# Gated attention plus S4 convolution on one core: a reordered prologue, zero fills by DMA, and new costs in the planner that writes the instruction orders

## The chip, the cores and the metric

The kernel runs on one core of one Trainium2 chip. The metric is the device time of one execution in microseconds (us); lower is better. The core has TensorE (PE, matmuls, with its weight loads shown apart as PEld), VectorE (DVE), ScalarE (ACT), GpSimd (POOL) and SyncE (SP). Each runs its own instruction stream in order and waits on semaphores. DMA transfers are issued from an engine's stream (here from SP) and run on 16 shared DMA engines.

## The reference: what is computed

```python
x = A_x                                              # (1, 2048, 448), bf16
g = sigmoid((x * gate_w).sum(-1, keepdims=True))
# A: attention, 16 query heads of 28, one shared key and value head
q, k, v = heads(x @ wq), x @ wk, x @ wv
a = concat(softmax(q @ k.T * 28 ** -0.5) @ v) @ wo
# B: a state-space (S4) convolution along the sequence, per channel d, 256 modes n
dt = exp(log_dt)
K[d, l] = Re sum_n C[d, n] * dt B[d, n] * exp(dt A[d, n] * l)
b = causal_conv(x, K) + x * Dskip                    # by FFT of length 4096
out = g * a + (1 - g) * b
```

## The kernel before

**Who sets the order.** The kernel does not issue its instructions where they stand in the code. Each `pg.op(engine, fn, ns, rd, wr, pr, ...)` notes an operation, its estimated duration `ns`, the keys it reads and writes, and a priority `pr` (smaller goes first). `Prog.schedule` (L113) then simulates the five engines: again and again it takes, of all operations whose inputs are ready, the one that can start first, and among equals the one with the smallest `pr`. This gives each engine a fixed order; `emit` adds the semaphore waits. `slack` is a delay that the planner adds before it holds an operation for ready; a `lock` guards a PSUM bank used in turn by several operations. A DMA is booked (L105) at packets x (30 + 0.03 x bytes) ns / 16 x 1.1, or packets x (105 + 0.022 x bytes) / 16 x 1.1 from 1500 bytes on, one after the other, then 2200 ns until it has landed; its issue takes 60 ns of the queue (L171). If a transfer lands later than planned, the engine that comes to it stands still with all that follows in its order.

**Prologue.** Four DMAs bring x into `tab` (key `xst`). PE transposes it in two halves (L475) through banks 0 to 3, ACT and DVE copy it to `xT` (L486, L488). ACT also writes the zeros of `U` (L393) and DVE those of `O` (L394) and of the padded weights (L384). `prep_params` (L493) makes the seeds of the S4 kernel: transposed parameters (L517), range reduction, sine and cosine by ACT (L535, L536), products (L523, the helper line of all of them). `prep_attn` (L562) makes `kT` (L571, L576), its largest magnitude (L579) and from that the column `Wb` that bounds the exponent (L585), the values (L592, L596) and the gates (L609, L615, L617, L620). A DMA (`omq`, L623) brings 1 - g into rows of 64, and PE mirrors and spreads them (L630). `qproj` (L638) makes the queries of one group of four heads: four matmuls (L649), absolute values (L655), the `Wb` matmul (L657), the copy to `qT` (L659).

**Attention.** 16 steps of (512 queries, 4 heads). For 1024 tiles PE makes scores (L915) in batches of 3 and 2, ACT takes the exponential (L925, 410 instructions), and PE multiplies by V (L933, "P.V", four matmuls of one key block). `norm` (L877) ends a step: DVE copies (L883), a DMA brings the row sums to `denT` (four pieces, L885), DVE inverts them (L888), they go through DRAM (`R_scratch`) and come back as `rdenB` (L890), and DVE multiplies (L892). `outp` (L850) makes the output projection.

**Convolution.** 28 chunks of 16 channels. DVE builds powers in `masters` (L694 to L709, once for four chunks) and `tables` (L722 to L757). `kgen` (L760) contracts them on PE (L773, four groups of 16 matmuls) in the bank `psX`, DVE copies to `kstg` (L783), and four DMAs write the kernel values to DRAM, `KP_scratch` (L786). For each of four channel quads, `tload` (L790) reads a Toeplitz layout of 1 MB back into one of three `T` buffers, and PE runs 8 steps of four matmuls (L829) against `U`, the blocks of x loaded by 48 DMAs (`uload`, L445). DVE takes the result to `cst` (L837), PE transposes it (L807), DVE adds it to `O` (L814). The convolution of a chunk is noted two chunks behind its kernel generation (`LAG`).

Of the kernel before, what the change touches and what calls it, by code (L numbers as in the profile page):

```python
# [11 lines left out]
P = 128  # L12
# [41 lines left out]
class Prog:  # L54
# [44 lines left out]
    def dma(self, pairs, desc, slot, rd=(), wr=(), pr=0, eng="sp", slow=False):  # L99
        kw = dict(allow_slow_non_contiguous=True) if slow else {}  # L100

        def fn(e):
            return [e.dma_start(o, i, **kw) for o, i in pairs]  # L103
        nd, size = desc
        o = self.op(eng, fn, nd * (30.0 + 0.03 * size if size < 1500 else 105.0 + 0.022 * size) / 16.0 * 1.1, rd, wr, pr)  # L105
        o.slot, o.ndma = slot, len(pairs)
        prev = self.slots.get(slot)
        if prev is not None:
            o.deps[prev] = 1
        self.slots[slot] = o.i  # L110
        return o

    def schedule(self):  # L113
# [19 lines left out]
        while done < n:  # L133
# [148 lines left out]
def el(n, rate=0.96, fix=62):  # L282
    return fix + n / rate


class Kernel:
# [10 lines left out]
    def build(self):  # L297
        nc = self.nc
        with self.es:
# [5 lines left out]
            self.prep_params()  # L305
            self.prep_attn()
            self.main()
# [4 lines left out]
    def alloc(self):  # L312
# [51 lines left out]
        self.KP = nc.dram_tensor("KP_scratch", (D * KPW,), BF).ap()  # L364
        self.R = nc.dram_tensor("R_scratch", (16 * 4 * 512,), F32).ap()

    def consts(self):
# [16 lines left out]
        ms = lambda buf, n, val, key: pg.op("dve", lambda e: e.memset(V(buf, 0, n), val), 60 + n / 3.8, wr=[key])  # L384
        ms(self.Wq, NT * 512, 0.0, "Wq")
        ms(self.Wk, NT * P, 0.0, "Wk")
        ms(self.Wo, NT * D, 0.0, "Wo")
        ms(self.Wb, P, 0.0, "Wb")
        pg.op("dve", lambda e: e.memset(self.vaug.v(0, P, 28, [[32, 16]]), 1.0), 80, wr=["va"])
        pg.op("dve", lambda e: e.memset(self.vaug.v(0, P, 29, [[32, 16], [1, 3]]), 0.0), 80, wr=["va"])  # L390
        pg.op("dve", lambda e: e.memset(V(self.zero, 0, 1), 0.0), 60, wr=["zero"])
        zz = self.zero.v(0, P, 0, [[0, 16 * D]])
        pg.op("act", lambda e: e.activation(self.U.v(0, P, 16 * D, [[1, 16 * D]]), zz, AF.Copy), 6200, rd=["zero"], wr=["Uz"])  # L393
        pg.op("dve", lambda e: e.memset(V(self.O, 0, 16 * D), 0.0), 3000, wr=["O"], pr=1)  # L394
# [6 lines left out]
        pg.op("dve", lambda e: e.memset(V(self.kstg, 0, 256), 0.0), 100, wr=[("kst", 0)])  # L401

    def loads(self):
# [3 lines left out]
        for hf in range(4):  # L407
            pg.dma([(xst.v(0, P, hf * 4 * D, [[D, 4], [1, D]]), dram(x, hf * 4 * P * D, [[D, P], [P * D, 4], [1, D]]))],
                   (512, 896), f"x{hf}", wr=[("xst", hf)], eng="sp")
# [4 lines left out]
        def lraw(k):  # L414
            pg.dma([(self.rawv(k, DT, 0, [[NM, 4], [1, NM]]), dram(ins[self.names[k]], 0, [[NM, DT], [DT * NM, 4], [1, NM]]))],
                   (448, 512), f"raw{k}", wr=[("raw", k)])
        pg.dma([(wks.v(0, DT, 0, [[DH, 4], [1, DH]]), dram(ins["A_wk"], 0, [[DH, DT], [DT * DH, 4], [1, DH]])),
                (self.Wv.v(0, DT, 0, [[32, 4], [1, DH]]), dram(ins["A_wv"], 0, [[DH, DT], [DT * DH, 4], [1, DH]]))],
               (896, 56), "wk", wr=["wks", "Wv"])
        pg.op("dve", lambda e: e.tensor_copy(self.Wk.v(0, DT, 0, [[32, 16], [1, DH]]),  # L420
                                             wks.v(0, DT, 0, [[DH, 4], [0, 4], [1, DH]])), 300, rd=["wks"], wr=["Wk", "rd"])
        lraw(0)
        lraw(1)
        pg.dma([(self.dt32.v(0, P, 0, [[1, D]]), dram(ins["B_log_dt"], 0, [[0, P], [1, D]]))], (128, 896), "ldt", wr=["dt"])
# [3 lines left out]
                                             wst.v(0, DT, 0, [[DH, 64], [1, DH]])), 1000, rd=["wqs"],  # L428
              wr=["Wq", ("acc", 0), ("acc", 1)])
# [3 lines left out]
        for k in range(2, 6):  # L433
            lraw(k)
# [3 lines left out]
        pg.dma([(dram(self.KP, 4 * S, [[4 * KPW, 112], [1, 256]]), self.kstg.v(0, 112, 0, [[1, 256]]))],  # L438
               (112, 512), "pad", rd=[("kst", 0)], wr=["pad"], eng="sp", pr=3)
# [5 lines left out]
    def uload(self):  # L445
        pg, x = self.pg, self.ins["A_x"]
        for k in range(3):
# [7 lines left out]
            pg.dma(lst, (1024, 896), f"u{k}", rd=["sw", "Uz"], wr=["U"], pr=2)  # L455
# [10 lines left out]
    def prep_x(self):  # L466
        pg = self.pg
        xst, xT = self.tab, self.xT
        for hf in range(2):
            for T in range(NT):  # L470
                t, o = self.bank(T, True)

                def mm(e, hf=hf, T=T, t=t, o=o, part=0):
                    for k in range(4 * part, 4 * part + 4):
                        r = e.matmul(t.v(0, DT, o + 128 * k, [[1, 128]]),  # L475
                                     xst.v(0, P, (8 * hf + k) * D + DT * T, [[1, DT]]),
                                     self.ident.v(0, P, 0, [[1, P]]), is_transpose=True, tile_position=(0, 0))
                    return r
                for part in range(2):
                    pg.op("pe", lambda e, mm=mm, part=part: mm(e, part=part), 450,  # L480
                          rd=[("xst", 2 * hf + part), "id"], wr=[("b", T)])
                dst = xT.v(0, DT, T * S + 1024 * hf, [[1, 1024]])
                src = t.v(0, DT, o, [[1, 1024]])
                key = f"xT{T}" + "ab"[hf]
                if T % 2 == 0:
                    pg.op("act", lambda e, d=dst, s=src: e.activation(d, s, AF.Copy), 1030, rd=[("b", T)], wr=[key], pr=-2)  # L486
                else:
                    pg.op("dve", lambda e, d=dst, s=src: e.tensor_copy(d, s), 700, rd=[("b", T)], wr=[key], pr=-2)  # L488

    def xk(self, col, c=None):  # L490
        return [f"xT{T}" + ("a" if col < 1024 else "b") for T in range(NT)]

    def prep_params(self):  # L493
        pg = self.pg
        fT, fO = self.T.cast(F32), self.U.cast(F32)
        W2 = 2 * D
        fb = lambda j: (fT, j * W2) if j < 6 else (fO, (j - 6) * W2)
        t = lambda j: fb(j)[0].v(0, P, fb(j)[1], [[1, W2]])
        tt = lambda j: fb(j)[0].v(0, P, fb(j)[1], [[D, 2], [1, D]])
        tc = lambda j: fb(j)[0].v(0, P, fb(j)[1], [[D, 2], [16, NCH], [1, 16]])  # L500
        f = fT
        K = lambda j: ("tp", j)
        allT = [("T", s) for s in range(self.NTR)]
        dtb = self.dt32.v(0, P, 0, [[0, 2], [1, D]])
        pg.op("act", lambda e: e.activation(f.v(0, P, 0, [[1, D]]), self.dt32.v(0, P, 0, [[1, D]]), AF.Exp), 600,
              rd=["dt"], wr=[K(0)], pr=1.3)
        pg.op("dve", lambda e: e.tensor_copy(self.dt32.v(0, P, 0, [[1, D]]), f.v(0, P, 0, [[1, D]])), 400,
              rd=[K(0)], wr=["dt"], pr=1.3)
        bk = {0: 4, 1: 5, 2: 6, 3: 4, 4: 5, 5: 6}

        def trans(k):
            t_, o = self.bank(bk[k], True)

            def mm(e):
                for half in range(2):
                    for T in range(4):
                        r = e.matmul(t_.v(0, P, o + half * D + DT * T, [[1, DT]]),  # L517
                                     self.rawv(k, DT, T * NM + 128 * half, [[1, 128]]),
                                     self.ident.v(0, DT, 0, [[1, DT]]), is_transpose=True, tile_position=(0, 0))
                return r  # L520
            pg.op("pe", mm, 800, rd=[("raw", k), "id"] + [("on", i) for i in range(2)], wr=[("b", bk[k])], pr=1.4)
            return t_.v(0, P, o, [[D, 2], [1, D]]), ("b", bk[k])
        TT = lambda e, o, a, b, op: e.tensor_tensor(o, a, b, op)  # L523
        ns = el(W2)
        p0, k0 = trans(0)
        p1, k1 = trans(1)
        pg.op("dve", lambda e: TT(e, tt(0), p0, dtb, ALU.mult), ns, rd=[k0, "dt"], wr=[K(0)] + allT, pr=1.3)
        pg.op("dve", lambda e: TT(e, tt(1), p1, dtb, ALU.mult), ns, rd=[k1, "dt"], wr=[K(1)], pr=1.3)
        pg.op("act", lambda e: e.activation(t(0), t(0), AF.Exp), 950, rd=[K(0)], wr=[K(0)], pr=1.3)
        pg.op("dve", lambda e: e.tensor_scalar(t(2), t(1), 1.0 / TWO_PI, MAGIC, ALU.mult, ALU.add), ns / 2, rd=[K(1)], wr=[K(2)], pr=1.3)  # L530
        pg.op("dve", lambda e: e.tensor_scalar(t(2), t(2), -MAGIC, -TWO_PI, ALU.add, ALU.mult), ns / 2, rd=[K(2)], wr=[K(2)], pr=1.3)
        pg.op("dve", lambda e: TT(e, t(1), t(1), t(2), ALU.add), ns, rd=[K(1), K(2)], wr=[K(1)], pr=1.3)
        pg.op("dve", lambda e: e.tensor_scalar(t(1), t(1), -math.pi, math.pi, ALU.max, ALU.min), ns / 2, rd=[K(1)], wr=[K(1)], pr=1.3)
        pg.op("dve", lambda e: e.scalar_tensor_tensor(t(2), t(1), -1.0, t(1), ALU.mult, ALU.max), ns, rd=[K(1)], wr=[K(2)], pr=1.3)
        pg.op("act", lambda e: e.activation(t(3), t(1), AF.Sin), 2000, rd=[K(1)], wr=[K(3)], pr=1.3)  # L535
        pg.op("act", lambda e: e.activation(t(4), t(2), AF.Sin, bias=self.small.v(0, P, 3, [[1, 1]]), scale=-1.0), 950,  # L536
              rd=[K(2), "hpi"], wr=[K(4)], pr=1.3)
# [505 lines left out]
```

## Time and profile before

| what | value |
|---|---|
| median of 3 runs | 688.93 us (688.78 to 693.11) |
| profiled execution | 698.53 us |
| its span, first to last instruction | 696.7 us |
| mean granted TensorE clock | 0.813 |
| DMA moved | 133.79 MB, of it 112 T loads of 1024 KB |

One execution was traced; all rows come from it. In groups of instructions the columns are the line, engine, operation, output <- inputs and shapes, count, busy us, mean ns of one, then the idle time before them and what ended it. In the timeline, "x16" merges neighbours of one kind, and the bracket gives the engine's idle time before and its releaser. "Windows" give each engine's busy time in a stretch, with the granted clock, the DMA engines' busy share and GB/s. Times of the timeline count from the first instruction. SPq is SyncE's queue, whose rows are DMA issues; all DMAs share the helper line L103.

### The profile page before, as it was taken

What the parts mean: (1) busy time and instruction counts of PE and PEld (TensorE: products, weight loads), DVE (VectorE), ACT (ScalarE), POOL (GpSimd) and SP (SyncE); (2) the same over time, 40 slices, a digit from 0 to 9 for tenths busy, and PEclk for the clock granted to TensorE, in tenths of its full rate; (3) what the DMA queues carried; (4) which work ended last, traced back from release to release, by engine and by line L of the source; (5) the groups of instructions that cost most, each with busy time, mean ns of one, the idle gap of its engine ahead of it and who ended that gap; (6) DMA issues with size and microseconds to landing.
All of it is one profiled execution on the core that took longest, in us unless ns stands there. A gap on an engine that the chain in (4) does not pass through costs nothing.

```text
span 696.7 us, 18695 instructions
## 1 busy us (share of the span) xinstructions
PE 527.4 (76%) x8275; PEld 256.9 (37%) x8290; DVE 531.6 (76%) x1153; ACT 506.3 (73%) x431; POOL 2.1 (0%) x14
## 2 busy tenths in 40 slices
PE   6546787887879878779878868887788887877623
PEld 4311243244434444334444434334343443443101
DVE  6969988987989879977889897797789887821101
ACT  8529887876888868867778767876777886767830
POOL 1000000000000000000000000000000000000000
PEclk9855697598988989787899988769898998987555
DMA  9123374478726676366755856357771387778003
GB/s 215 30 57 82 99 244 188 170 246 291 270 70 236 239 270 247 128 230 218 264 196 187 294 212 223 104 205 251 258 276 29 127 273 282 252 254 321 19 16 107
DMA packets 44217, 133.79 MB, mean 192 GB/s; under 512 B 13176, under 2 KB 27752, under 8 KB 29800
## 3 DMA queue, kind: packets, MB, share of 16 engines
q1 hardware_dynamic: 44136, 132.59, 55.9%
q8 instruction: 65, 1.06, 0.6%
q14 instruction: 16, 0.13, 0.1%
HBM read 128.57 MB, written 3.86 MB: 190 GB/s over the span
## 4 chain that ended last, share of the span: by engine, by line
DMA 35%; PE 28%; DVE 20%; ACT 7%; SPq 7%; issue 1%; ACTq 0%
DMA T<-KP_scratch 19%; PE psS L829 8%; DMA denT<-acc 7%; PE psS L915 7%; SPq L103 7%; ACT expT L925 6%; PE psX L773 6%; PE psB L933 4%; DMA R_scratch<-denT 3%; DMA KP_scratch<-kstg 3%; DVE tab L734 2%; DVE tmp L737 2%; DMA rdenB<-R_scratch 2%; DVE tab L742 2%; DVE tmp L752 1%
## 5 line engine op out<-in xcount | busy, mean ns | idle before, releaser
L925 ACT ACTIVATE expT<-psS 128x1536 bf16<-128x1536 f32 (+1 forms) x410 | 483.9, 1236 | 150.8 <-PE psS L915 130.7
L829 PE MATMUL psS<-T,U 128*32 128x128 bf16 (+7 forms) x3584 | 153.6, 309 | 66.6 <-DMA T<-KP_scratch 58.7
L915 PE MATMUL psS<-qT,kT 29*128 29x512 bf16 x1024 | 182.8, 454 | 13.7 <-ACT expT L925 9.5
L933 PE MATMUL psB<-expT,vaug 128*32 128x512 bf16 x1024 | 123.6, 468 | 37.5 <-ACT expT L925 36.2
L829 PEld LDWEIGHTS psS<-T,U 128*32 128x32 bf16 (+7 forms) x3584 | 103.1, 155 | 118.7 <-DMA T<-KP_scratch 78.5
L915 PEld LDWEIGHTS psS<-qT,kT 29*128 29x128 bf16 x1024 | 39.0, 93 | 131.8 <-issue 100.3
L734 DVE TENSOR_TENSOR tab<-tab,mbf 128x128 bf16<-128x128 bf16 (+4 forms) x140 | 78.3, 563 | 0.5
L742 DVE TENSOR_TENSOR tab<-tab,tmp 128x128 bf16<-128x128 bf16 (+4 forms) x140 | 78.3, 564 | 0.5
L737 DVE TENSOR_TENSOR tmp<-tab,mbf 128x128 bf16<-128x128 bf16 (+4 forms) x140 | 78.4, 564 | 0.0
L773 PE MATMUL psX<-tab 128*32 128x64 bf16 x1792 | 65.8, 294 | 5.2 <-DVE O L814 2.3
L933 PEld LDWEIGHTS psB<-expT,vaug 128*32 128x32 bf16 x1024 | 31.3, 107 | 76.7 <-ACT expT L925 67.3
L773 PEld LDWEIGHTS psX<-tab 128*32 128x32 bf16 x1792 | 48.3, 139 | 24.3 <-issue 13.5
L750 DVE TENSOR_TENSOR tab<-tab,mbf 128x2048 bf16<-128x2048 bf16 x28 | 34.1, 1217 | 0.1
L757 DVE TENSOR_TENSOR tab<-tab,tmp 128x2048 bf16<-128x2048 bf16 x28 | 34.0, 1216 | 0.0
L752 DVE TENSOR_TENSOR tmp<-tab,mbf 128x2048 bf16<-128x2048 bf16 x28 | 34.0, 1216 | 0.0
L837 DVE TENSOR_TENSOR cst<-psS,omq 128x512 bf16<-128x512 f32 x28 | 19.3, 688 | 19.2 <-PE psS L829 19.2
L783 DVE CAST kstg<-psX 128x256 bf16<-128x256 f32 x28 | 11.8, 422 | 26.2 <-PE psX L773 25.9
L883 DVE TENSOR_TENSOR acc<-psB,grow 128x512 f32<-128x512 f32 x16 | 11.0, 688 | 26.3 <-PE psB L933 26.2
L706 DVE TENSOR_TENSOR mbf<-mst,sgn 128x256 bf16<-128x256 f32 x70 | 29.3, 418 | 0.0
L888 DVE RECIPROCAL denT<-denT 128x16 f32<-128x16 f32 x16 | 4.0, 252 | 31.0 <-DMA denT<-acc 31.0
L694 DVE TENSOR_TENSOR msq<-mst 128x256 f32<-128x256 f32 x63 | 26.4, 418 | 0.0
L892 DVE TENSOR_TENSOR onT<-acc,rdenB 128x512 bf16<-128x512 f32 x16 | 11.1, 691 | 17.3 <-DMA rdenB<-R_scratch 17.3
(106 smaller groups left out, 309.3 us busy)
## 6 DMA issues: line engine op xcount, KB each, us to landing
T<-KP_scratch SPq DMA_DIRECT2D x112, 1024.0 KB, 7.8
rdenB<-R_scratch SPq DMA_DIRECT2D x64, 64.0 KB, 2.2
U<-in_A_x_dram SPq DMA_DIRECT2D x48, 56.0 KB, 2.2
tab<-in_A_x_dram SPq DMA_DIRECT2D x4, 448.0 KB, 5.2
KP_scratch<-kstg SPq DMA_DIRECT2D x112, 16.0 KB, 1.6
out_dram<-O SPq DMA_DIRECT2D x16, 112.0 KB, 1.8
denT<-acc SPq DMA_DIRECT2D x64, 2.0 KB, 4.5
acc<-in_A_wq_dram SPq DMA_DIRECT2D x1, 392.0 KB, 6.8
```

Source lines behind the costliest of these rows:

```text
L103: return [e.dma_start(o, i, **kw) for o, i in pairs]
L734: pg.op("dve", lambda e, d=dst3, a=src, m=m, w=w: e.tensor_tensor(d, a, mbf.v(0, P, m, [[HC, 4], [0, w], [1, HC]]), ALU.mult), el(n, 1.92) ...
L737: pg.op("dve", lambda e, a=src, m=m, w=w: e.tensor_tensor(tmp.v(0, P, so, [[w * HC, 4], [HC, w], [1, HC]]), a, mbf.v(0, P, m + 128, [[HC, ...
L742: pg.op("dve", lambda e, d=d2, t=t2: e.tensor_tensor(d, d, t, ALU.add), el(n, 1.92), rd=[("tmp", s), ("tab", s, lv + 1)], wr=[("tab", s, l ...
L750: pg.op("dve", lambda e: e.tensor_tensor(dst, src, mbf.v(0, P, m, [[HC, 2], [0, 32], [1, HC]]), ALU.mult), el(n, 1.92), rd=rk + mk, wr=[(" ...
L752: pg.op("dve", lambda e: e.tensor_tensor(tmp.v(0, P, so, [[BLK, 2], [HC, 32], [1, HC]]), src, mbf.v(0, P, m + 64, [[HC, 2], [0, 32], [1, H ...
L757: pg.op("dve", lambda e: e.tensor_tensor(d2, d2, t2, ALU.add), el(n, 1.92), rd=[("tmp", s), ("tab", s, 6)], wr=[("tab", s, 6)], pr=pr)
L773: r = e.matmul(self.psX.v(32 * g, 32, 64 * jj, [[1, 64]]), tab.v(0, P, to + (4 + comp) * BLK + o, [[HC, 32]]), tab.v(0, P, to + comp * BLK ...
L829: r = e.matmul(ps.v(32 * j, 33 - m, po + 128 * k, [[1, 128]]), self.U.v(0, P, (m - 1) * D + 4 * gi + j, [[D, 33 - m]]), self.T.v(0, P, s * ...
L915: r = e.matmul(self.psS.v(0, P, 1536 * s + 512 * k, [[1, 512]]), kT.v(32 * h, DH + 1, 128 * kt, [[1, 128]]), qT.v(32 * h, DH + 1, 512 * qs ...
L925: pg.op("act", lambda e: e.activation(expT.v(0, P, 512 * (i0 % 10), [[1, n]]), self.psS.v(0, P, 1536 * s, [[1, n]]), AF.Exp, scale=SQ), 17 ...
L933: r = e.matmul(self.psB.v(32 * h, 32, 0, [[1, 512]]), vaug.v(0, P, 32 * kt, [[1, 32]]), expT.v(0, P, 512 * ((4 * st + h) % 10), [[1, 512]] ...
```

## The change

- **Planner.** An issue takes 450 instead of 60 ns of its queue; `dma` accepts a duration, and a T load is booked at 3300 ns (the formula gave 2512). The first matmul of each T buffer gets 2500 ns of slack; the inversion and the last product of `norm` 5000 ns, but for the last step; the `omq` mirror on PE 4000 ns. Exponentials are booked 75 + n/1.2 with 160 ns behind them (172 + n/1.2, 60), P.V 390 ns (330), a convolution step 112 (90).
- **Ranks.** Scores 0.5 to -0.5 (P.V stays at 0); convolution 4 to 2.5, so ahead of kernel generation (3), whose four groups become eight of half the size with the same matmuls.
- **Prologue.** x is transposed and projected in quarters, each with two copies (ACT and DVE) through four banks; the k projection uses banks 4 and 5. The sine part of the seeds (parameter 1, range reduction, both sines) comes before `prep_attn`; the rest waits for the first q. The first q follows directly. Gates go through bank 7 one by one, also after the first q. `Wb` starts as -1 in four column blocks and is scaled in one operation instead of four.
- **Loads.** x first; the loads of wk, log_dt and parameter 1 are issued from ACT; wq comes before the other parameters.
- **Zero fills.** A 2 KB line of zeros in DRAM (`Z`), written beside the padding of KP, is read 896 times into `O` and 448 times into the zero part of `U`; the fills by ACT and DVE go. The fill of `Wo` moves from DVE to POOL. The U loads also wait for the fill of U.
- **Fewer DMAs.** The four writes of `kgen` and the four `denT` reads of `norm` become one DMA each.

```diff
-    def dma(self, pairs, desc, slot, rd=(), wr=(), pr=0, eng="sp", slow=False):
+    def dma(self, pairs, desc, slot, rd=(), wr=(), pr=0, eng="sp", slow=False, ns=None):
...
-                free[e] = r + 60.0 * o.ndma
+                free[e] = r + 450.0 * o.ndma
...
             self.prep_x()
-            self.prep_params()
+            self.seeds_sin()
             self.prep_attn()
+            self.qproj(0, 0)
+            self.seeds()
+            self.prep_gate()
             self.main()
...
-        pg.op("act", lambda e: e.activation(self.U.v(0, P, 16 * D, [[1, 16 * D]]), zz, AF.Copy), 6200, rd=["zero"], wr=["Uz"])
-        pg.op("dve", lambda e: e.memset(V(self.O, 0, 16 * D), 0.0), 3000, wr=["O"], pr=1)
+        ms(self.Wo, NT * D, 0.0, "Wo", "pool")
...
+        pg.dma([(dram(self.KP, 4 * S, [[4 * KPW, 112], [1, 256]]), self.kstg.v(0, 112, 0, [[1, 256]])),
+                (dram(self.Z, 0, [[256, 4], [1, 256]]), self.kstg.v(0, 4, 0, [[1, 256]]))],
+               (112, 512), "pad", rd=[("kst", 0)], wr=["pad"], pr=3)
+        pg.dma([(self.O.v(0, P, 0, [[1024, 7], [1, 1024]]), dram(self.Z, 0, [[0, P], [0, 7], [1, 1024]]))],
+               (896, 2048), "oz", rd=["pad"], wr=["O"], pr=4)
...
+        pg.dma([(bass.AP(tensor=self.U.h, offset=16 * D, ap=[[2 * self.U.rs, 64], [1024, 7], [1, 1024]]),
+                 dram(self.Z, 0, [[0, 64], [0, 7], [1, 1024]]))], (448, 2048), "uz", rd=["pad", "sw"], wr=["U"], pr=2)
...
-        for hf in range(2):
-            for T in range(NT):
-                t, o = self.bank(T, True)
+        for hf in range(4):
+            for j in range(2):
+                bk = 2 * (hf % 2) + j
+                t, o = self.bank(bk, True)
...
+        pg.op("pe", mo, 200, rd=["anti", ("kst", 1)], wr=[("b", 5)], pr=1.7, slack=4000)
...
-        pg.dma([(dram(self.KP, (4 * c + g) * 4 * KPW, [[256, 32], [1, 256]]),
-                 self.kstg.v(32 * g, 32, ks * 256, [[1, 256]])) for g in range(4)],
+        pg.dma([(dram(self.KP, 16 * c * KPW, [[4 * KPW, 4], [256, 32], [1, 256]]),
+                 self.kstg.v(0, P, ks * 256, [[1, 256]]))],
                (128, 512), f"kw{ks}", rd=[("kst", ks)], wr=[("KP", c)], pr=0)
...
-               (128, 8192), f"T{s}", rd=[("KP", c), "pad"], wr=[("T", s)], pr=1)
+               (128, 8192), f"T{s}", rd=[("KP", c), "pad"], wr=[("T", s)], pr=1, ns=3300)
...
-                pg.op("pe", mm, 90, rd=[("T", s), "U"], wr=[X, ("cst", cs)] + ([("b", 5)] if c == 0 else []) if first else [X], pr=4,
-                      lock="C" if first else None)
+                pg.op("pe", mm, 112, rd=[("T", s), "U"], wr=[X, ("cst", cs)] + ([("b", 5)] if c == 0 else []) if first else [X], pr=2.5,
+                      lock="C" if first else None, slack=2500 if m == 1 else 0)
...
-        pg.dma([(self.denT.v(32 * h, 32, 16 * a, [[1, 16]]), acc.v(32 * h + 28, 1, 512 * a, [[16, 32], [1, 16]])) for h in range(4)],
+        far = 0 if i == 15 else 5000
+        pg.dma([(self.denT.v(0, P, 16 * a, [[1, 16]]),
+                 bass.AP(tensor=acc.h, offset=28 * acc.rs + 512 * a, ap=[[32 * acc.rs, 4], [16, 32], [1, 16]]))],
                (128, 64), f"dn{a}", rd=[("acc", a)], wr=[("dn", a)], pr=0)
...
-            pg.op("pe", mm, 330, rd=sorted(rd, key=str), wr=bk, pr=0.5)
+            pg.op("pe", mm, 330, rd=sorted(rd, key=str), wr=bk, pr=-0.5)
...
-                                                AF.Exp, scale=SQ), 172 + n / 1.2, rd=bk, wr=[("e", (i0 + k) % 10) for k in range(len(ts))], pr=0)
+                                                AF.Exp, scale=SQ), 75 + n / 1.2, rd=bk, wr=[("e", (i0 + k) % 10) for k in range(len(ts))], pr=0, lat=160)
```

More of the change, by code (lines that the diff above doesn't have):

```diff
@@ L507, in prep_params @@
[L507 to L522, printed above, removed]
@@ L531, in prep_params @@
[L531 to L534, printed above, removed]
@@ L589, in mv, with prep_gate @@
+    def prep_gate(self):
+        pg = self.pg
+        xT = self.xT
         def mv(e):
@@ L892, in norm @@
         pg.op("dve", lambda e: e.tensor_tensor(self.onT.v(0, P, 512 * (i % 8), [[1, 512]]), av, self.rdenB.v(0, P, 0, [[1, 512]]), ALU.mult),
-              el(512), rd=[("acc", a), "rd"], wr=[("on", i % 8)], pr=3)
+              el(512), rd=[("acc", a), "rd"], wr=[("on", i % 8)], pr=3, slack=far)
     def main(self):
@@ L936, in mm @@
                 return r
-            pg.op("pe", mm, 330, rd=["va"] + [("e", (4 * st + h) % 10) for h in range(4)], wr=[("b", 6)], pr=0,
+            pg.op("pe", mm, 390, rd=["va"] + [("e", (4 * st + h) % 10) for h in range(4)], wr=[("b", 6)], pr=0,
                   slack=600 if kt == 0 else 0)
```

257 lines of the change are left out of this document (141 added, 116 removed).

## The prediction

> **What bounds the kernel now.** I read the page's busy shares first, then the windows by stage.
>
> ```profile
> PE 527.4 (76%) x8275; PEld 256.9 (37%) x8290; DVE 531.6 (76%) x1153; ACT 506.3 (73%) x431; POOL 2.1 (0%) x14
> ...
> 0.00:33.00 33.00, 20.29 (x155) 12.85 (x156) 26.60 (x48) 21.76 (x20) 2.09 (x14) 0.95 0.60 129
> 33.00:52.00 19.00, 7.87 (x94) 3.12 (x92) 12.68 (x40) 5.30 (x6) 0.00 (x0) 0.50 0.20 51
> 52.00:87.00 35.00, 25.09 (x205) 6.58 (x198) 34.41 (x82) 31.01 (x27) 0.00 (x0) 0.59 0.33 90
> 87.00:650.00 563.00, 454.85 (x7710) 227.96 (x7722) 452.63 (x977) 431.25 (x365) 0.00 (x0) 0.85 0.63 219
> 650.00:697.00 47.00, 19.29 (x124) 6.37 (x122) 5.24 (x9) 17.00 (x16) 0.00 (x0) 0.57 0.15 46
> ```
>
> No engine is full. The columns are PE, PEld, DVE, ACT, POOL, then clock, DMA share and GB/s. In the long stretch 87 to 650 us the three engines are busy 77 to 81% each, so their floors lie close together and the time is made by them waiting for each other. In 33 to 52 us hardly anything runs. The list of waits says for what:
>
> ```profile
> ACT expT L925 <- PE psS L915: 130.7, 149, 4.7
> ...
> PE psS L829 <- DMA T<-KP_scratch: 58.7, 47, 4.9
> ...
> DVE denT L888 <- DMA denT<-acc: 31.0, 15, 3.7
> ...
> DVE kstg L783 <- PE psX L773: 25.9, 14, 4.4
> ...
> ACT expT L925 <- PE psB L933: 17.6, 5, 13.3
> DVE onT L892 <- DMA rdenB<-R_scratch: 17.3, 10, 4.9
> ...
> PE psB L630 <- DMA kstg<-omg: 9.7, 1, 9.7
> DVE omq L635 <- PE psB L630: 6.3, 1, 6.3
> ```
>
> ACT starves for scores (130.7 us), but the scores stand in PE's fixed order behind convolution matmuls that wait for T (58.7 us). DVE stands at two small DMAs (31.0 + 17.3 us) and at late kernel-generation matmuls (25.9 us). The planner that wrote the orders booked these transfers shorter than they are:
>
> ```profile
> DMA to landing us min/median/max: 5.4/7.8/11.4
> ```
>
> That is T. The old planner books 128 packets of 8192 B at 2.5 us and adds 2.2: 4.7 us, below the fastest of 112 loads. So PE is sent to T early nearly each time.
>
> **The head, step by step.** The timeline of the first 55 us:
>
> ```profile
> 3.54 6.17 ACT L393 ACTIVATE U<-zero 128x7168 bf16<-128x7168 bf16 x1 [1.46 <-DVE zero L391]
> 4.49 3.04 DVE L394 MEMSET O<- 128x3584 uint32 x1 [0.69 <-issue]
> 8.20 0.95 PEld L475 LDWEIGHTS psS<-ident,tab 128*112 128x112 bf16 x8 [0.49 <-DMA tab<-in_A_x_dram]
> 8.23 1.06 PE L475 MATMUL psS<-ident,tab 128*112 128x128 bf16 x8 [0.32 <-DVE xT L488]
> 9.62 3.75 ACT L486 ACTIVATE xT<-psS 112x1024 bf16<-112x1024 bf16 x4
> 12.60 3.61 PE L571 MATMUL psS<-xT,Wk 112*128 112x512 bf16 x16
> 16.56 0.68 DVE L579 TENSOR_REDUCE small<-kT 128x1 f32<-128x512 bf16 x1
> 23.96 0.68 DVE L659 CAST qT<-psX 128x512 bf16<-128x512 f32 x1
> 33.17 4.62 ACT L925 ACTIVATE expT<-psS 128x1536 bf16<-128x1536 f32 x4
> 37.58 11.18 SPq L103 DMA_DIRECT2D U<-in_A_x_dram  x16
> 39.51 0.29 DVE L704 CAST mbf<-seedz 128x256 bf16<-128x256 f32 x1
> 48.81 0.61 SPq L103 DMA_DIRECT2D kstg<-omg  x1
> 50.68 0.28 PE L630 MATMUL psB<-kstg,anti 32*128 32x64 bf16 x2 [9.71 <-DMA kstg<-omg]
> 52.10 2.36 ACT L925 ACTIVATE expT<-psS 128x1536 bf16<-128x1536 f32 x2 [13.34 <-PE psB L933]
> ```
>
> The last part of x is in at 8.2 us, the first q is ready at 24.6 us (23.96 + 0.68), the first exponential starts at 33.2 us. The quarter pipeline makes the chain from 8.2 us: 16 transposes at 1.06/8 each 2.1, copy 0.94 (3.75/4), projection of one quarter 0.9 (3.61/4), its copy and maximum 0.7 each (the maximum's 0.68 for both), two tiny operations 0.3, the Wb matmul 0.6, cast 0.7, scores 0.6: together 7.5, so 15.7 us. I add 2 us for sine operations standing ahead on DVE and for Wq's landing: first exponential near 18 us, 15 us earlier. With ACT's 13.3 us hole gone, the exponentials gain 28 us.
>
> DVE's stream gains less. From first q (24.6) to the first master (39.5) it has 14.9 us of work; some 3 us of sine steps move ahead of q, so masters start near 17 + 12 = 29 us, 10 us earlier, and the 6.3 us wait for omq goes. **Head: 16 us** on DVE, whose tables feed the convolution, and 28 on ACT. I take the smaller, for both streams must end.
>
> Why the hole goes: `omq`'s DMA stood on SP behind 16 U issues (11.2 us), and PE stood at L630 with 8 P.V matmuls behind it, on whose release ACT waited. Now the U loads also wait for the uz fill, and PE's consumer is planned 4 us late. If omq is again queued behind U issues, 11.2 less 4, some 7 us, comes back.
>
> The zero fills cost nothing where they go: O (1.8 MB) and U (0.9 MB) at the 219 GB/s of the stretch above are 8.4 and 4.2 us of transfer, and this row shows the DMA engines idle there:
>
> ```profile
> 20.00:30.00 10.00, 7.68 (x44) 3.84 (x45) 9.81 (x15) 4.57 (x5) 0.00 (x0) 0.83 0.02 6
> ```
>
> Without that cover uz would put U, and the first convolution, back by 4.2 us. That all read one 2 KB line is shown by no row; below, 0; above, four times as long (a guess), 50 us for both, still before the first convolution if issued by 20 us. I take nothing. The 6.2 and 3.0 us taken off ACT and DVE lie under the wait for x, so they count in the chain only. ACT's three new DMA issues (some 0.5 us each as on SP) fall before x's first landing. POOL's Wo fill (0.8 us on DVE) is due only before the Wo load.
>
> **The steady stretch.** A T load now books 0.45 issue + 3.3 + 2.2 us, and its first matmul another 2.5: 8.5 us against the measured median of 7.8 and longest of 11.4. Well over half of the loads are in by then. What late T costs beside the wait itself:
>
> ```profile
> 247.28 0.42 PE L933 MATMUL psB<-expT,vaug 128*32 128x512 bf16 x4
> ...
> 252.07 0.49 PE L829 MATMUL psS<-T,U 128*32 128x128 bf16 x8 [2.76 <-DMA T<-KP_scratch]
> 252.35 0.63 PE L933 MATMUL psB<-expT,vaug 128*32 128x512 bf16 x4
> ...
> 253.57 2.37 ACT L925 ACTIVATE expT<-psS 128x1536 bf16<-128x1536 f32 x2 [3.14 <-PE psS L915]
> ```
>
> After 2.8 us at T the same four P.V matmuls take 0.63 us where they took 0.42, and ACT lost 3.1 us. PE can win 58.7 us at most; DVE, whose two DMA waits also get 5 us of slack (48.3 us less 3.7 and 4.9 in the last norm, which keeps its order) and whose kgen waits follow PE's stalls (25.9), 65.6 us. I take six tenths of the smaller, **35 us**: the share of loads that I judge in time. Bounds: 0 (each early T only moves the wait elsewhere) and 58.7. The ranks (scores over P.V, convolution over kgen) and the kgen halves issue the same matmuls; I give them nothing, with 26 us (DVE's kstg wait doubled) as what a starved kgen would cost.
>
> The Trainium skill, "TensorE: Matmul & The Clock Gate", Part 1, says that PE runs at half clock until about 3.4 us of sustained work and falls back after such an idle stretch. The trace agrees (clock 0.50 at 33 to 52 us); by it, fewer stalls would also lift the 0.85 of the long stretch, a gain outside my sum.
>
> **Queues and tail.** KP writes go from four DMAs to one, denT reads too: SP issues 84 + 48 fewer.
>
> ```profile
> denT<-acc SPq DMA_DIRECT2D x64, 2.0 KB, 4.5
> ...
> KP_scratch<-kstg SPq DMA_DIRECT2D x112, 16.0 KB, 1.6
> ...
> 670.18 2.47 SPq L103 DMA_DIRECT2D denT<-acc  x4
> ```
>
> In the tail four issues took 2.47 us: one, **1.9 us** saved. Nowhere does the trace show these two as one DMA. Below: they land as now. Above: four times the 1.6 us. I take as now.
>
> **Sum** on the profiled execution: 698.5 (span 696.7 and 1.8 around it) - 16 - 35 - 1.9 = 645.6 us. The median of the runs, 688.9, is 0.986 of that execution: **636 us**.
>
> **Rivals.**
> *Full gain.* 28 + 58.7 + 1.9 off: 609.9, times 0.986: 601 us. For it: after each T wait PE is slow, so fewer waits pay twice. Against it: DVE's 531.6 us of work, the 42 it idles in the last 47, and 6 in the head make 580 already, which leaves 30 us for all waits of the long stretch, where DVE idles 110 now (563 - 452.6).
> *Head only.* The transfers set the pace: T is 112 MB, DMA is 63% busy, a faster stretch makes each landing later, and loads only wait elsewhere. 698.5 - 16 - 1.9 = 680.6, times 0.986: 671 us. Against it: the fastest load takes 5.4 us, so the median holds 2.4 us of queueing that better spacing can spare.
> *Slower: narrow writes.* The merged KP write, whose outer dimension is now 4, runs on four engines instead of sixteen and lands after 4 x 1.6 = 6.4 us where the plan has 2.6. The first T of each of 28 chunks is then 3.8 us late, less 0.7 of margin: 87 us of PE stalls, against which the saved 35 and 18 stand: 698.5 - 53 + 87 = 732.5; with six tenths of the stalls on the path, 698, times 0.986: 688 to 722, say 700 us. It decides once the write lands over 5 us. Against it: T's own loads keep 128 outer rows.
> The Trainium skill, "DMA: Bandwidth & Descriptors", "Why a DMA increments its semaphore by 16 and not by 1", states this rule: the number of engines must divide the slowest dimension of both sides. No run here shows it yet.
> *No change.* The planner's fixed orders drift from the chip as before and the head's gain is waited away at the end: 689 us.
>
> **How the numbers follow.** Forecast 0.47, own range 618 to 655; full gain 0.16; head only 0.20; slower 0.11; no change 0.06. The runs before spread to 0.6%, so over 1% can be told. Faster 0.47 + 0.16 + 0.20 = 0.83, same 0.06, slower 0.11. The range, 600 to 686, reaches from full gain to past head only; it leaves out the slower case, no change, and the fastest few of full gain, in all about 0.2.
>
> **What would show it.** Right: first exponential at 16 to 20 us; no ACT hole over 5 us before 60; the first convolution matmul 14 to 20 us before its 87.6; PE's wait for T near 24 us; DVE's for denT and rdenB under 20; one denT issue in the tail. Wrong: KP writes landing over 5 us; PE's wait for T still near 59; or T landing later than 9 us in the median.
>
> ```profile
> L829 PE MATMUL psS<-T,U x3584: 273/303/368, 87.6 to 648.9; 128*32 128x128 bf16 x25, 128*24 128x128 bf16 x25, 128*30 128x128 bf16 x25, 128*22 128x128 bf16 x25
> ```

## The result and the profile after

The changed kernel takes 598.82 us (median of 4, 596.56 to 600.11) beside 690.68 us for the kernel before on the same chip: ratio 0.8665, 95% interval 0.8621 to 0.8709. The forecast was 636, the range 600 to 686: the direction was right, the gain (92 us) nearly twice the forecast's 53, and the time just below the range. The profiled execution spans 597.3 us. Of the runs below, one execution each of e2 (664.22 us), g4 (611.92) and k1 (1040.48) counts as slow; the medians have them, the ratios leave them out.

The page's shares and the list of waits of the changed kernel (line numbers shift: L829 is now L853, L915 L941, L925 L951, L933 L959, L883 L907, L888 L914, L892 L918):

```profile
PE 508.3 (85%) x8290; PEld 258.7 (43%) x8290; DVE 523.7 (88%) x1152; ACT 492.8 (83%) x431; POOL 3.7 (1%) x15
```

```profile
PE psS L941 <- ACT expT L951: 29.0, 58, 6.0
...
ACT expT L951 <- PE psS L941: 22.5, 34, 5.8
...
PE psS L853 <- DMA T<-KP_scratch: 14.8, 6, 3.8
...
DVE onT L918 <- DMA rdenB<-R_scratch: 10.7, 1, 10.7
...
DVE denT L914 <- DMA denT<-acc: 4.9, 1, 4.9
...
DVE kstg L807 <- PE psX L797: 2.9, 4, 1.2
```

ACT's wait for scores fell from 130.7 to 22.5 us, PE's for T from 58.7 to 14.8. What DVE still waits for denT and rdenB is one wait each, in the last norm. PE's 36.2 us before P.V for the exponential are gone (0.4); PE now waits 29.0 (9.5) before the scores instead.

The same 440 us of the middle in both kernels, windows 100 to 540 (PE, PEld, DVE, ACT, POOL, clock, DMA share, GB/s), before first:

```profile
100.00:540.00 440.00, 355.13 (x5888) 175.95 (x5896) 377.36 (x830) 338.34 (x288) 0.00 (x0) 0.84 0.61 212
```

```profile
100.00:540.00 440.00, 402.74 (x7140) 211.41 (x7136) 432.09 (x932) 410.83 (x357) 0.00 (x0) 0.94 0.72 248
```

DVE is busy 98% of it, ACT 93%, PE 92%, at a granted clock of 0.94 instead of 0.84.

Two streams run through the kernel, attention and convolution, and one row of each tells where it starts and ends: the copy that closes each of 16 attention steps, and the convolution matmuls. Instructions on the tiles `acc` and `T`, before and after:

```profile
L883 DVE TENSOR_TENSOR acc<-psB,grow x16: 681/691/692, 82.2 to 669.5; 128x512 f32<-128x512 f32 x16
```

```profile
L907 DVE TENSOR_TENSOR acc<-psB,grow x16: 669/681/705, 72.7 to 547.1; 128x512 f32<-128x512 f32 x16
```

```profile
L853 PE MATMUL psS<-T,U x3584: 274/301/368, 100.1 to 585.3; 128*32 128x128 bf16 x25, 128*24 128x128 bf16 x25, 128*30 128x128 bf16 x25, 128*22 128x128 bf16 x25
```

Before, the convolution ran 87.6 to 648.9 and attention ended last: 27.2 us of normalisation, projection and stores followed its 669.5. Now attention closes at 547.1, its tail lies under the convolution, and only 12.0 us follow the last convolution matmul at 585.3. By the convolution's marks the 99.4 us of span are: +12.5 until its first matmul, -76.1 in the 28 chunks (561.3 to 485.2), -35.8 behind it (47.8 to 12.0).

The head, in the timeline of the changed kernel:

```profile
14.71 1.06 PE L486 MATMUL psS<-ident,tab 128*112 128x128 bf16 x16
...
16.83 0.62 DVE L428 COPY Wq<-acc 112x1792 bf16<-112x1792 bf16 x1
...
24.57 1.45 ACT L951 ACTIVATE expT<-psS 128x1536 bf16<-128x1536 f32 x1 [5.83 <-PE psS L941]
...
26.04 1.28 ACT L544 ACT_TABLE_LOAD   x1
...
28.30 1.28 ACT L562 ACT_TABLE_LOAD   x1
...
30.56 1.28 ACT L545 ACT_TABLE_LOAD   x1
...
32.91 1.28 ACT L951 ACT_TABLE_LOAD   x1
...
34.21 3.28 ACT L951 ACTIVATE expT<-psS 128x1024 bf16<-128x1024 f32 x3
...
39.61 0.27 DVE L729 CAST mbf<-seedz 128x256 bf16<-128x256 f32 x1
...
86.68 0.60 SPq L103 DMA_DIRECT2D KP_scratch<-kstg  x1
...
89.29 1.87 SPq L103 DMA_DIRECT2D T<-KP_scratch  x3
```

The last quarter of x is transposed at 14.7 us, not at 8.2. Most of that is its landing. The last of the four x loads is issued at 2.4 us in both kernels; from issue to landing it took, before and after:

```profile
DMA to landing us min/median/max: 8.1/8.1/8.1
```

```profile
DMA to landing us min/median/max: 10.7/10.7/10.7
```

So it is in at 10.5 us before (the row at 8.20, read as the last part, is the third quarter) and at 13.1 after. That the three loads which ACT now issues between 0.8 and 2.4 us slow it is likely, but not shown. The rest is PE's order, in which the last quarter's transposes stand behind two quarters' k projections. The first exponential comes at 24.6 (18 forecast, 33.2 before). Then the seeds' exponential falls between the two sines, ACT loads four tables and does no second exponential of the scores until 34.2. The first master is at 39.6, where it was at 39.5. The first merged KP write had landed at most 2.6 us after the start of its issue, when T's first load was issued; before it was 2.8 (78.66 to 81.45). The convolution starts 12.5 us later all the same: 5.1 of it are there when DVE begins the first chunk's last table step (L775 at 75.9 us, L750 at 70.8 before), 2.9 more come up to the KP write, and 4.5 between that write and the first convolution matmul (13.4 us, 8.9 before).

### The profile page after: what moved, and what is told of

Its sections match the earlier page's. It is cut to its first block, busy times and chain, and to the rows that moved or that the text cites. A ratio compares the mean times of both kernels' runs of the same rounds, so it can differ in the third digit from the quotient of the medians.

```text
span 597.3 us, 18611 instructions
## 1 busy us (share of the span) xinstructions
PE 508.3 (85%) x8290; PEld 258.7 (43%) x8290; DVE 523.7 (88%) x1152; ACT 492.8 (83%) x431; POOL 3.7 (1%) x15
## 4 chain that ended last, share of the span: by engine, by line
DVE 57%; PE 23%; ACT 13%; DMA 5%; issue 1%; SPq 0%; ACTq 0%
ACT expT L951 12%; DVE tab L759 8%; DVE tab L767 8%; DVE tmp L762 8%; PE psS L941 7%; PE psS L853 4%; PE psB L959 4%; DVE tab L775 4%; DVE tab L782 4%; DVE tmp L777 4%; DVE mbf L731 3%; PE psX L797 2%; DVE msq L719 2%; DVE cst L861 2%; DVE mbf L729 2%; PE psX L674 1%
## 5 line engine op out<-in xcount | busy, mean ns | idle before, releaser
L951 ACT ACTIVATE expT<-psS 128x1536 bf16<-128x1536 f32 (+1 forms) x410 | 473.9, 1249 | 41.3 <-PE psS L941 22.5
L941 PE MATMUL psS<-qT,kT 29*128 29x512 bf16 x1024 | 173.0, 425 | 32.6 <-ACT expT L951 29.0
L853 PE MATMUL psS<-T,U 128*32 128x128 bf16 (+7 forms) x3584 | 152.2, 304 | 17.0 <-DMA T<-KP_scratch 14.8
L853 PEld LDWEIGHTS psS<-T,U 128*32 128x32 bf16 (+7 forms) x3584 | 112.5, 152 | 46.9 <-issue 21.6
L959 PE MATMUL psB<-expT,vaug 128*32 128x512 bf16 x1024 | 111.0, 427 | 0.4 <-ACT expT L951 0.4
L941 PEld LDWEIGHTS psS<-qT,kT 29*128 29x128 bf16 x1024 | 38.6, 92 | 128.5 <-ACT expT L951 94.9
L759 DVE TENSOR_TENSOR tab<-tab,mbf 128x512 bf16<-128x512 bf16 (+4 forms) x140 | 78.3, 562 | 0.6
L767 DVE TENSOR_TENSOR tab<-tab,tmp 128x1024 bf16<-128x1024 bf16 (+4 forms) x140 | 78.0, 562 | 0.7
L762 DVE TENSOR_TENSOR tmp<-tab,mbf 128x512 bf16<-128x512 bf16 (+4 forms) x140 | 78.4, 562 | 0.0
L959 PEld LDWEIGHTS psB<-expT,vaug 128*32 128x32 bf16 x1024 | 26.5, 95 | 68.2 <-issue 65.5
L775 DVE TENSOR_TENSOR tab<-tab,mbf 128x2048 bf16<-128x2048 bf16 x28 | 34.1, 1217 | 0.0
L674 PE MATMUL psX<-xT,Wq 112*128 112x512 bf16 x64 | 20.0, 444 | 0.6 <-DVE kstg L807 0.6
L918 DVE TENSOR_TENSOR onT<-acc,rdenB 128x512 bf16<-128x512 f32 x16 | 10.9, 683 | 10.7 <-DMA rdenB<-R_scratch 10.7
L729 DVE CAST mbf<-mst 128x256 bf16<-128x256 f32 x70 | 19.9, 285 | 0.1
L722 DVE TENSOR_TENSOR mst<-msq 128x128 f32<-128x128 f32 x70 | 19.7, 281 | 0.0
## 6 DMA issues: line engine op xcount, KB each, us to landing
O<-Z_scratch SPq DMA_DIRECT2D x1, 1792.0 KB, 13.3
```

Of the source, the lines that this page charges most:

```text
L759: pg.op("dve", lambda e, d=dst3, a=src, m=m, w=w: e.tensor_tensor(d, a, mbf.v(0, P, m, [[HC, 4], [0, w], [1, HC]]), ALU.mult), el(n, 1.92) ...
L762: pg.op("dve", lambda e, a=src, m=m, w=w: e.tensor_tensor(tmp.v(0, P, so, [[w * HC, 4], [HC, w], [1, HC]]), a, mbf.v(0, P, m + 128, [[HC, ...
L767: pg.op("dve", lambda e, d=d2, t=t2: e.tensor_tensor(d, d, t, ALU.add), el(n, 1.92), rd=[("tmp", s), ("tab", s, lv + 1)], wr=[("tab", s, l ...
L775: pg.op("dve", lambda e: e.tensor_tensor(dst, src, mbf.v(0, P, m, [[HC, 2], [0, 32], [1, HC]]), ALU.mult), el(n, 1.92), rd=rk + mk, wr=[(" ...
L853: r = e.matmul(ps.v(32 * j, 33 - m, po + 128 * k, [[1, 128]]), self.U.v(0, P, (m - 1) * D + 4 * gi + j, [[D, 33 - m]]), self.T.v(0, P, s * ...
L941: r = e.matmul(self.psS.v(0, P, 1536 * s + 512 * k, [[1, 512]]), kT.v(32 * h, DH + 1, 128 * kt, [[1, 128]]), qT.v(32 * h, DH + 1, 512 * qs ...
```

## The experiments

Theory P: the planner's prices are the cause. Booked too short, a T load made PE stand at T with scores and P.V behind, and that spread to ACT and DVE. Rivals: H, the head; R, the ranks; D, the merged DMAs; later I, the issue price alone, and F, that DVE's own work is now the bound. Each run is compared with the kernel before on its own chip; "att" is the last attention copy, "conv" the last convolution matmul in its profiled execution. Before: att 669.5, conv 648.9, span 696.7; after: 547.1, 585.3, 597.3. Where the text compares two runs with each other, it takes their medians; these come from several chips, so the ratios are given where they say something else.

| run | median us | ratio, 95% interval | att | conv | span |
|---|---|---|---|---|---|
| e1_steady_alone | 596.38 | 0.857 (0.853 to 0.861) | 558.9 | 583.9 | 595.7 |
| e2_prologue_alone | 658.10 | 0.941 (0.935 to 0.948) | 632.4 | 615.8 | 657.2 |
| e3_no_slack | 596.71 | 0.857 (0.854 to 0.860) | 555.5 | 582.8 | 594.6 |
| e4_old_ranks | 618.45 | 0.889 (0.884 to 0.893) | 561.4 | 604.1 | 616.0 |
| g4_four_dmas | 606.47 | 0.871 (0.863 to 0.878) | 548.2 | 588.5 | 600.1 |
| h1_issue60 | 600.43 | 0.866 (0.864 to 0.869) | 551.2 | 586.3 | 598.3 |
| n2_old_T_price | 625.71 | 0.900 (0.894 to 0.906) | 588.9 | 609.7 | 626.2 |
| g1_merges_only | 662.56 | 0.954 (0.946 to 0.961) | 629.6 | 608.6 | 654.6 |
| g2_durations_only | 627.94 | 0.906 (0.899 to 0.913) | 606.9 | 607.5 | 633.1 |
| g3_ranks_only | 691.91 | 0.996 (0.992 to 0.999) | 661.6 | 638.9 | 688.7 |
| k1_issue450_only | 673.52 | 0.971 (0.966 to 0.976) | 643.8 | 614.8 | 670.2 |
| k2_engine_times_only | 680.39 | 0.982 (0.976 to 0.987) | 655.6 | 637.8 | 681.9 |
| k3_neutral | 695.73 | 1.004 (1.001 to 1.006) | 667.7 | 643.4 | 694.0 |
| k5_T3300_only | 631.15 | 0.907 (0.899 to 0.915) | 601.7 | 585.2 | 627.7 |
| n1_T3300_and_ranks | 624.58 | 0.901 (0.894 to 0.908) | 592.1 | 586.4 | 618.5 |
| m1_less_dve_after | 586.11 | 0.842 (0.836 to 0.848) | 549.0 | 573.5 | 585.4 |
| m2_less_dve_before | 678.43 | 0.975 (0.967 to 0.984) | 650.6 | 592.8 | 677.3 |
| m4_sines_together | 596.53 | 0.857 (0.850 to 0.863) | 553.7 | 582.0 | 593.9 |

### The two halves

The kernel before with all of the change but prologue, loads and fills; and the changed kernel with the planner's part undone:

```diff
 # e1_steady_alone, from before: new prices, slacks, ranks, merged DMAs
+                free[e] = r + 450.0 * o.ndma
+               (128, 8192), f"T{s}", rd=[("KP", c), "pad"], wr=[("T", s)], pr=1, ns=3300)
...
 # e2_prologue_alone, from after: the same lines back, merges kept
-                free[e] = r + 450.0 * o.ndma
+                free[e] = r + 60.0 * o.ndma
```

> The kernel before, with its old prologue, loads and fills, but with all of the change's planner costs, slacks, ranks, the split kernel generation and the merged DMAs. Theory P (the time came from planning DMA results late enough, so that DVE hardly stands still between 100 and 585 us): most of the 92 us, 605 to 630 us, DVE's waits for denT and rdenB under 12 us before the tail. Rival H (the earlier first exponential puts attention ahead of the convolution, and this does it): 650 to 680 us.

> The changed kernel with the planner's costs, slacks and ranks as before (issue 60 ns, T load by the formula, no extra slack, scores 0.5, convolution 4, kernel generation in four); prologue, zero fills and merged DMAs stay. Theory P: 665 to 695 us, with 40 us or more of PE's waits for T. Rival H: 600 to 640 us.

Without the new prologue: 596.4 us, at least as fast as the whole change, and below the range that theory P gave. Its first convolution matmul stands at 87.5, where before had it. The head is worth nothing here, and H falls. The other half brought 38 us, between the two theories' ranges; the merged DMAs, which it kept, bring 32 alone (below).

### One part undone in the changed kernel

```diff
 # e3_no_slack
-                      lock="C" if first else None, slack=2500 if m == 1 else 0)
+                      lock="C" if first else None, slack=None)
-        far = 0 if i == 15 else 5000
+        far = None
 # e4_old_ranks
-            ... wr=bk, pr=-0.5)      # scores;  convolution pr=2.5
+            ... wr=bk, pr=0.5)       #          convolution pr=4
 # g4_four_dmas: KP write and denT read in four pieces again
 # h1_issue60
-                free[e] = r + 450.0 * o.ndma
+                free[e] = r + 60.0 * o.ndma
 # n2_old_T_price
-               ... f"T{s}", ..., pr=1, ns=3300)       # and slack=2500 if m == 1 else 0
+               ... f"T{s}", ..., pr=1)                # and slack=500
```

> The changed kernel with only the added slack of the T matmuls and of norm back at the old defaults (0.5 us at convolution steps, 0 and 0.3 us in norm); new durations, ranks and prologue stay. Theory P: the slack is the core of it, 630 to 660 us, DVE's waits for denT and rdenB back at 25 to 45 us. If the durations (issue 450 ns, T 3300 ns) do it without slack: 600 to 615 us. Rival H: within 10 us of 599.

> The changed kernel with the old ranks alone: scores 0.5 behind P.V, convolution 4 behind kernel generation. Theory P: 595 to 610 us. Rival R (the ranks feed ACT and DVE, and this is the steady stretch's gain): 635 to 670 us with ACT's wait for scores back over 80 us.

> The changed kernel with both merges undone: four KP writes and four denT reads again, each booked at 450 ns of issue. Theory D: 620 to 640 us. Theory P or R: 595 to 608 us.

> The changed kernel with the planner's DMA issue back at 60 ns; all else of the change stays. Theory I (the issue price is the one that mattered, since each issue holds SP some 0.5 us): 620 to 640 us. Rival E (the engines' durations and the T price carry it, and merged DMAs already mend SP's queue): 597 to 607 us.

> The changed kernel with the T load booked by the old formula (2512 ns) and the old slack of 500 ns at each convolution step; issue price, engine durations, ranks, merges and prologue stay. If the T price carries the gain by itself: 630 to 650 us, PE's wait for T over 35 us. If the other parts stand in for it, as they did for the issue price: 600 to 612 us.

The slack, which I had taken for the core of the gain, is worth nothing (596.7). The issue price neither (600.4). Undoing the merges costs 8 us by the medians and 3 by the ratios, whose intervals overlap. The ranks cost 20 us when undone, and the T price together with T's slack 27 (by the ratios 15 and 23), both between the two theories' ranges. The waits of e4 and of n2 tell the two apart:

```profile
ACT expT L951 <- PE psS L941: 49.1, 95, 5.8
...
PE psB L959 <- ACT expT L951: 36.2, 63, 1.3
...
PE psS L853 <- DMA T<-KP_scratch: 17.6, 9, 2.9
```

```profile
ACT expT L951 <- PE psS L941: 53.4, 57, 5.8
...
PEld psS L853 <- DMA T<-KP_scratch: 50.2, 44, 3.2
PE psS L853 <- DMA T<-KP_scratch: 42.1, 39, 3.5
```

With the old ranks T is on time (17.6 us), but PE stands 36.2 us at P.V for the exponential, as before. With the old T price the wait for T is back (42.1 us on PE), with everything else of the change in place but T's slack. The slack alone is worth nothing (e3); the old price with the new slack was not run, nor was the changed kernel with its engine durations put back.

### One part alone on the kernel before

```diff
 # g1_merges_only: one KP write, one denT read
 # g2_durations_only: issue 450, T 3300, exponential 75 + n/1.2 (lat 160), P.V 390, convolution 112
 # g3_ranks_only: scores -0.5, convolution 2.5, kernel generation in eight
 # k1_issue450_only: issue 450          # k2_engine_times_only: exponential, P.V, convolution
 # k5_T3300_only
-               (128, 8192), f"T{s}", rd=[("KP", c), "pad"], wr=[("T", s)], pr=1)
+               (128, 8192), f"T{s}", rd=[("KP", c), "pad"], wr=[("T", s)], pr=1, ns=3300)
 # n1_T3300_and_ranks: k5 and g3 together
 # k3_neutral
-    SEM_NS = 60
+    SEM_NS = 61
```

> The kernel before with the four KP writes and the four denT reads each merged to one DMA, nothing else. Theory D (fewer issues on SP let the T loads go out on time; the prologue run at 658 us kept these merges): 650 to 670 us. Theory P (durations) and theory R (ranks): 680 to 695 us. If one merged write ran on few engines and hurt: over 700 us.

> The kernel before with the change's booked durations alone (issue 450 ns, T load 3300, exponential 75 + n/1.2 and 160 behind, P.V 390, convolution step 112), no new rank, slack or merge. Theory P: 610 to 640 us, PE's wait for T under 25 us. Theory R or D: 665 to 690 us.

> The kernel before with the ranks alone (scores -0.5, convolution 2.5, kernel generation in eight pieces), old durations, slack and four DMAs. Theory R: 640 to 665 us, PE's wait at P.V for the exponential (36.2 us before) under 5. Theory P or D: 675 to 695 us.

> The kernel before with the issue booked at 450 instead of 60 ns, one number changed. Theory I: 635 to 660 us. Rival E: 675 to 695 us.

> The kernel before with the new durations of exponential, P.V and convolution alone; issue, T load, ranks and slack as before. Theory I: 680 to 700 us. Rival E: 640 to 665 us.

> The kernel before with the planner's semaphore delay at 61 instead of 60 ns: a change without a meaning, that gives another order. All theories: within 8 us of the kernel before. If a new order alone moves the time by 20 us or more, the single-number runs beside it can't be read one by one.

> The kernel before with the T load booked at 3300 instead of 2512 ns, one number changed. If the three new prices add up to the 66 us that all of them gave (20 for the issue, 13 for the engines): 655 to 668 us. If they only work together: 675 to 695 us.

> The kernel before with two edits: the T load booked at 3300 ns, and the new ranks (scores -0.5, convolution 2.5, kernel generation in eight). The T price alone gave 631 us, the ranks alone 692. If the ranks pay once T is planned in time: 600 to 615 us. If they need the other durations: 625 to 640 us.

One new order without a meaning moved the time by 0.4% (k3), so steps of several per cent can be read; the ranks alone (0.996) can't be told from such a step, and the engine times alone (0.982) hardly. One number, the T load at 3300 instead of 2512 ns, gives 62 us: more than was expected of it and as much as all new durations together (627.9 and 631.2, overlapping intervals). Shares, waits and streams of that run:

```profile
PE 502.0 (80%) x8275; PEld 255.6 (41%) x8290; DVE 528.0 (84%) x1153; ACT 502.6 (80%) x431; POOL 2.1 (0%) x14
```

```profile
ACT expT L925 <- PE psS L915: 67.2, 108, 2.1
...
PE psB L933 <- ACT expT L925: 33.4, 55, 1.3
...
PE psS L829 <- DMA T<-KP_scratch: 19.5, 26, 2.0
...
DVE denT L888 <- DMA denT<-acc: 11.4, 9, 3.7
...
DVE kstg L783 <- PE psX L773: 8.1, 5, 5.3
```

PE's wait for T fell by 39.2 us (58.7 to 19.5), and its busy time for the same matmuls by 25.4 (527.4 to 502.0) at a clock of 0.892 instead of 0.813: together 64.6 of the 69.0 us of span by PE's account. The Trainium skill, "TensorE: Matmul & The Clock Gate", Part 1, has PE drop to half clock after an idle stretch of some 3.4 us and need as long a busy one to return; these two runs agree in that fewer stalls went with a higher clock. But stalls are not all that sets the clock here. In the changed kernel from 36 to 87 us, ahead of the first convolution matmul, PE is busy 91% of the time and waits 0.6 us at most, yet the granted clock is 0.55; in the window 100 to 540 above, 92% busy went with 0.94. Its waits in that stretch, then the stretch itself:

```profile
PE psS L941 <- ACT expT L951: 4.5, 11, 0.6
```

```profile
36.00:87.00 51.00, 46.36 (x279) 10.84 (x275) 45.45 (x122) 43.64 (x41) 0.00 (x0) 0.55 0.31 77
```

So how much of the 25.4 us the stalls themselves cost stays open.

k5's convolution ends at 585.2, as early as the whole change's. What it lacks is in attention, which closes at 601.7 and drags its 26 us behind it. In n1 the ranks move attention forward by another 9.6 us, but n1's profile is that of its fastest execution; in time they bring 7 us, less than I had expected, and the intervals (0.894 to 0.908, 0.899 to 0.915) overlap. With the rest of the prices, slacks and merges attention comes ahead of the convolution (e1: 558.9). Which of these does it is open: slack, issue price and merges could each be taken out of the changed kernel with attention still closing at 548 to 556.

The merges alone are worth 32 us. All DMA issues on SP together took 245.2 us before and 173.9 in g1 (added up from the traces), and PE's wait for T fell from 58.7 to 39.7 us in g1's profiled execution, its fastest (656.31 us). DVE's wait for denT, 31.0 us before, in g1:

```profile
DVE denT L890 <- DMA denT<-acc: 7.5, 8, 2.0
```

No run merges the KP writes or the denT reads alone, so the share of each is open.

### Is DVE now the floor?

The last addition of each chunk's tables (34.0 us on DVE) left out of both kernels, so the convolution's numbers lack one product term; and a version of e3 meant to set ACT's two sines side by side:

```diff
 # m1_less_dve_after, m2_less_dve_before
-        pg.op("dve", lambda e: e.tensor_tensor(d2, d2, t2, ALU.add), el(n, 1.92),
-              rd=[("tmp", s), ("tab", s, 6)], wr=[("tab", s, 6)], pr=pr)
 # m4_sines_together, from e3
-        ... AF.Exp), 950, rd=[K(0)], wr=[K(0)], pr=-0.5)
+        ... AF.Exp), 950, rd=[K(0), K(4)], wr=[K(0)], pr=-0.5)
```

> The changed kernel without the last addition of each chunk's tables (28 DVE operations of 1.22 us, 34.0 us; the convolution kernel is left wrong by one product term). Theory F (DVE, busy nearly without a break from 40 to 541 us, is now what sets the time, so all other savings end there): 565 to 578 us. Rival W (the time is still made of waits between engines): 585 to 597 us.

> The kernel before without the same 28 additions (34.0 us of DVE). Theory F: DVE was not the bound there, 675 to 690 us. Rival W, if DVE set the pace before as well: 655 to 665 us.

> The changed kernel without the added slack (596.7 us) and with the exponential of the seeds after both sines instead of between them, so that ACT loads two tables fewer (2 x 1.28 us). Theory F: the seeds come some 2 us earlier on DVE, 592 to 596 us. If the head doesn't count: 596 to 598 us.

F in this form falls: 34 us less DVE work saved 12.7 us after (some 17 by the ratios) and 15.1 before (693.47 to 678.43). The window 100 to 540 of m1 shows why it wasn't more:

```profile
100.00:540.00 440.00, 399.14 (x7234) 213.26 (x7244) 401.33 (x895) 407.33 (x354) 0.00 (x0) 0.96 0.75 256
```

DVE falls to 91% and ACT, at 93%, does no more exponentials than before (attention closes at 549.0, 547.1 with the full work). In the changed kernel the three engines' busy times lie within some 30 us of each other in these 440, and I read that as a common floor, not DVE's alone. No run lightened ACT or PE, so this is not shown.

m4 doesn't answer its question. ACT took an exponential of the scores between the two sines (L544, L545) and loaded four tables, as many as in e3 and the changed kernel; in the head of m4:

```profile
26.31 1.28 ACT L544 ACT_TABLE_LOAD   x1
...
28.57 1.28 ACT L951 ACT_TABLE_LOAD   x1
...
30.91 1.28 ACT L545 ACT_TABLE_LOAD   x1
...
33.26 1.28 ACT L951 ACT_TABLE_LOAD   x1
```

It ends where e3 does; what table loads in the head cost stays open. e1, e3 and m4 are the fastest of the kernels that compute all (596.4 to 596.7 us), 2 us under the changed kernel by the medians and 1% by the ratios.

## Why the prediction was wrong

**What bounds the kernel.** Right: T booked at 4.7 us, below the fastest load of 5.4, sent PE to T early, and scores stood behind it. k5 shows it by this one price, n2 by the price and T's slack. The planner books transfers one behind the other, so a longer T also moves those behind it: in k5 DVE's waits for denT and rdenB fell too (31.0 to 11.4 and 17.3 to 6.6 us), at their old prices. No run tells the two effects apart. One reading was too strong: from 33 to 52 us, where hardly anything was to run, DVE was busy 12.68 of 19 us.

**The head, 16 us.** Wrong, and worth nothing. The first master came at 39.6 instead of 29 us and the first convolution matmul 12.5 us later than before. The chain began at 8.2 us, but the last part of x landed at 10.5 us even before and at 13.1 after, a delay that the forecast put at nothing. The chain also left out that PE's order would set the last quarter's transposes behind two projections, and that the seeds' exponential would take ACT's table between the sines. The omq hole did go (no wait for it in the list), yet e1, with a hole of 14.3 us still there (its longest ACT wait at P.V), ends at the same time. Its attention closes 11.8 us later than the changed kernel's, but still under the convolution, which ends at 583.9 and 585.3 us.

**The steady stretch, 35 us.** This is the step that failed: by the convolution's marks it became 76.1 us. The six tenths were not the fault, for the wait for T fell by 39.2 us in k5 and by 43.9 in the changed kernel. The step took the smaller of two engines' waits and set the clock outside the sum; in k5 PE's busy time fell by 25.4 us more. And it gave the ranks nothing and merged DMAs nothing. Undone in the changed kernel the ranks cost 20 us, and with them came back a wait that I hadn't looked up (PE at P.V, 36.2 us). That wait is not the whole account of it: g3 took it down to 1.0 us with no gain in time, T still being late (50.7 us), and n1 to 1.2 us for those 7 us. Merged DMAs alone give 32 us. Each issue holds SP (0.59 us for a denT piece) with T loads and denT behind it, and the tail's 1.9 us was the only place where I had counted that.

**The tail.** The sum let attention end last, as it did. Attention finished 40 us ahead of the convolution's last step and its tail of 27 us went under: 35.8 us off the end, 1.9 in my sum. Both streams had to be followed to their ends, each with its own tail. Term by term the sum's 16, 35 and 1.9 us were -12.5, 76.1 and 35.8 us: the head's miss of 28.5 us hid part of the 75.0 that the other two fell short.

**The rivals.** Full gain gave the time (601) with 0.16, but by the head's 28 us and all of T's waits, which is not how it came: that it hit the time is luck. Head only fell with T landing sooner, not later (median 6.7 us; 7.8 before). Narrow writes fell: g1 is faster, and SP waited as long for the one merged KP write as for four, before and in g1:

```profile
SPq L103 <- DMA KP_scratch<-kstg: 41.5, 19, 5.1
```

```profile
SPq L103 <- DMA KP_scratch<-kstg: 39.8, 19, 5.0
```

The rule of the Trainium skill, "DMA: Bandwidth & Descriptors", "Why a DMA increments its semaphore by 16 and not by 1", may hold for the number of engines, which no row here shows; on these 64 KB and 8 KB it costs nothing measurable.

**Open.** The parts do not add. Alone, T price (62), merges (32), issue price (20), engine times (13) and ranks (2) make 129 us, and all of them together, with the slacks (e1), some 100. Which of them fills which gap was not followed instruction by instruction; nor why lightening DVE by 34 us moved the convolution's end by 56 us in the kernel before (m2) while attention's moved by 19.

## What to carry to other kernels

Where a planner writes the order, hold each booked transfer against its fastest measured landing: one that is booked below it makes every consumer early, and correcting one number alone gave 62 us here, where the whole change gave 92. Follow each stream to its own end with its own tail before summing; the tail of the one that ends first is free. And undo parts of a finished change as well as trying them alone: the slack and the issue price looked like the cause and could be taken out for nothing.

## What the hardware showed unexpectedly

DMA issues are work on SP's queue. Four issues of a denT read took 2.47 us, one takes 0.59, and 132 issues fewer took 32 us off the kernel at the same 133.8 MB moved. The fill of `O` from one 2 KB line landed 13.3 us after its issue, where 1.8 MB at 219 GB/s had been estimated at 8.4; nothing waited for it. The fill of `U`, issued at 38.2 us, took 7.9 us instead of 4.2; SP waited 7.2 us for it, and the U loads began at 46.1 us instead of 37.6.
